# Zero-padded 128x128 operands for the 64-row tails of two attention heads, with an earlier place for a final check

## The chip, the cores and the metric

The kernel runs on one core of one Trainium2 chip. The metric is the device time of one execution in microseconds. TensorE (PE, with its weight loads shown as PEld), VectorE (DVE), ScalarE (ACT) and GpSimd (POOL) each work through their own list of instructions in order and wait for each other through semaphores; DMAs are issued from SyncE's queue (SP).

## The reference

Two blocks follow each other, all in float32. The first is attention with 8 batches, 8 heads, 576 positions and a head size of 64, in which every query keeps only its 32 largest scores. The second is a feed-forward block on the 4608 rows of 512 that come out of it.

```python
scores = scale * np.matmul(q, k.transpose(0, 1, 3, 2))
kth = np.partition(scores, -top_k, axis=-1)[..., -top_k:-top_k + 1]
scores = np.where(scores >= kth, scores, -1000000000.0)
attn = softmax(scores)                      # exp, divided by its sum
x = (attn @ v) as rows of 8 * 64
...
h = x @ w_in                                # 512 -> 1024
solu = h * softmax(h)
ln = (solu - mean) / sqrt(var + 1e-6) * g_ln
out = ln @ w_out                            # 1024 -> 512
```

## The kernel before

The work is cut by pairs of heads. A pair has two heads of 64, so both lie on the 128 partitions, head 0 on partitions 0 to 63 and head 1 on 64 to 127. The 576 positions of a head are four main chunks of 128 (`NM = 4`) and a **tail of 64** (`ST`). The two heads' tails of queries make one tile of 128 rows, so one step has nine tiles of 128 query rows by 576 keys: two for each of four main chunks, and one for the tails of a pair. There are 32 steps, four for each batch, and 32 pairs, four for each batch.

The keys of a pair are prepared once: `load_k` (L664) loads the main keys `km` and the two tails `qt` and `kt`, each with 64 positions on partitions and both heads side by side; `prep_t` (L701) turns the two tails around on PE, `prep_tc` (L711) copies the result to the keys `kT` on ACT (L712, L713); `prep_k` and `prep_kc` do the main keys, `moments` and `moments_c` a matrix from which the spread of the scores is estimated. `load_v` (L678) loads the values, their tails `vt` with head 0 on partitions 0 to 63 and head 1 on 64 to 127.

In a step, `spread` (L782) makes the small products for that estimate, `scores` (L850) the scores in PSUM (`s_ps`, two buffers of two banks), `evac` copies them to SBUF on ACT. Three rounds of counting on DVE and ACT (`count0`, `count1`, `count2`) close in on each row's threshold, `nearest`, `best` and `kth` (L985) find it exactly, `exps`, `keep` and `norm` make the weights, `transpose_p` and `transpose_last` turn them around on PE, `copy_p`, `copy_pt` and `copy_last` bring them to SBUF as `PT`, and `attn_v` (L1083) multiplies them by the values, in two parts: part 0 has 320 query columns (two main chunks and a tail), part 1 has 256. `copy_v` puts the result in place for the feed-forward block: `mm1` (L1117), `hexp`, `solu`, `square`, `ln`, `transpose_ln`, `copy_ln`, `mm2` (L1176), `store` (L1184).

All products that concern heads work on a part of TensorE's array. A main score product contracts 64 rows and fills 128 columns; in the profile's form that is `64*128`, and the two heads' products lie on different halves of the rows. A product of `attn_v` is `128*64`, the two heads on different halves of the columns. The tail products of `scores`, `attn_v` and `spread` are `64*64`, head 0 on one corner of the array and head 1 on the opposite one. A float32 product shows as two records in the trace, a transpose and a bfloat16 product as one.

The order is written out by hand. Every operation is entered with a due time (`at`), from tables: `step_times` (L1199) for a step, `early_times` (L1235) in its place for the first four steps, `key_times` (L1372) for the pairs (the first batch apart), `first_times`, `token_times` and `last_times` for the feed-forward block, `weights_times` (L1463) for the 16 chunks of 128x512 weights. These weights come as 64-bit floats; `load_w`, `w_bits` (DVE), `w_low` (ACT), `w_mul` and `w_add` (POOL) make float32 of them near the start, and `w_again` (a second load), `w_exp` (DVE) and `w_check` (ACT, L631) look near the end whether their exponents were in range. Sorted by due time, the tables give the order of each engine's list (L1546); a due time has no other effect.

Last come a check and a branch: six reductions on DVE (L1557, to `hit` and `ok`) count whether every row met its conditions and every weight its range, a small product and two operations on one number (L1562 to L1568) make one flag of that, `bad`. Every engine loads it, and only if it is set does a general version of the kernel run (L1580).

Lines of the score and value products that can't be said in a sentence:

```python
s = big[0][h * ST : (h + 1) * ST] if tail else big[h]
...
lhsT=vm[:, h, c, :] if c < NM else vt[hd, :],
rhs=pt[:, h * NM + c, :] if c < NM else pt[hd, 2 * NM, :],
start=(c == 0), stop=(c == NM),
```

Of the kernel before, what the change touches and what calls it, by code (L numbers as in the profile page):

```python
# [8 lines left out]
F32 = mybir.dt.float32  # L9
# [434 lines left out]
def fast_path(  # L444
# [98 lines left out]

    def trunc(ap):

        return ap.bitcast(BF16)[:, 1::2]
# [117 lines left out]
    def load_k(n):  # L664
# [9 lines left out]
        for nm, src in (("q", q), ("k", k)):  # L674
            d[nm + "t"] = p1.tile([ST, 2, D], F32, tag=nm + "t", name=nm + "t")
            nc.sync.dma_start(out=d[nm + "t"], in_=src[b, hh, SM:S, :].rearrange("h p d -> p h d"))

    def load_v(n):  # L678
# [3 lines left out]
        t = p4.tile([2 * ST, D], F32, tag="vt", name="vt")  # L682
        nc.sync.dma_start(out=m, in_=v[b, hh, 0:SM, :].rearrange("h (p t) d -> p h t d", t=NM))
        for h in range(2):
            nc.sync.dma_start(out=t[h * ST : (h + 1) * ST, :], in_=v[b, 2 * hp + h, SM:S, :])
        ks[n]["v"] = (m, t)

    def kT_of(n):

        return once(  # L690
            ks[n], "kT", lambda: p4.tile([P, S + 2 * ST], F32, tag="kT", name="kT")
        )
# [8 lines left out]
    def prep_t(n):  # L701

        d = ks[n]
        pre = pre_of(n)
        for m, nm in enumerate("qk"):
            nc.tensor.transpose(
                pre[:, m * ST : (m + 1) * ST], d[nm + "t"].rearrange("p h d -> p (h d)"),
                ident[0:ST, 0:ST],
            )

    def prep_tc(n):  # L711
        nc.scalar.copy(out=kT_of(n)[:, 0 : 2 * ST], in_=ks[n]["pre"][:, 0 : 2 * ST])  # L712
        nc.scalar.copy(out=kT_of(n)[:, S + ST : S + 2 * ST], in_=ks[n]["pre"][:, ST : 2 * ST])  # L713
# [13 lines left out]
    def prep_kc(n):  # L727

        nc.scalar.activation(
            out=kT_of(n)[:, 2 * ST : S + ST], in_=ks[n]["tp"], func=AF.Copy,  # L730
            accum_out=mom_of(n)[:, D : D + 1],
        )

    def moments(n):
        d = ks[n]
        tm = d["tm"] = pre_of(n)[:, 2 * ST : 2 * ST + D]
# [34 lines left out]
    def queries_of(i, c):  # L771

        return keys_of(i, c)["kT"][:, 0:ST] if c == NM else st[i]["qT"][:, c * P : (c + 1) * P]
# [8 lines left out]
    def spread(i):  # L782
# [5 lines left out]
        for c in range(NM + 1):  # L788
            for h in range(2):
                hd = slice(h * D, (h + 1) * D)  # L790
                nc.tensor.matmul(
                    out=d["yt"][h * ST : (h + 1) * ST, :] if c == NM else d["ym"][:, c, h, :],
                    lhsT=trunc(queries_of(i, c)[hd, :]), rhs=trunc(keys_of(i, c)["mom"][hd, :]),
                    start=True, stop=True,
                )

# [53 lines left out]
    def scores(i, t):  # L850
# [3 lines left out]
        tail = t == NM  # L854
        js = [2 * t] if tail else [2 * t, 2 * t + 1]
        big = [ps_big.tile([P, 2, 512], F32, tag="big", name="s_ps") for _ in js]

        for half in range(2):
            for h in range(2):
                hd = slice(h * D, (h + 1) * D)  # L860
                s = big[0][h * ST : (h + 1) * ST] if tail else big[h]

                k0 = ST + half * SH + (ST if h == 0 or tail else 0)
                nc.tensor.matmul(  # L864
                    out=s[:, half, 0:SH], lhsT=queries_of(i, t)[hd, :], rhs=kT[hd, k0 : k0 + SH],
                    start=True, stop=True,
# [170 lines left out]
    def pt_of(i, part):  # L1037

        return once(
            st[i], ("PT", part),  # L1040
            lambda: p2.tile([P, 2 * NM + 1, SP], F32, tag="PT", name="PT"),
# [41 lines left out]
    def attn_v(i, part):  # L1083
        o = st[i]["om", part] = ps_o.tile([P, 512], F32, tag="o", name="om")

        for n, cols in runs_of(i, part):
            vm, vt = keys_of(i, n)["v"]
            pt = pt_of(i, part)[:, :, cols]
            for c in range(NM + 1):
                for h in range(2):  # L1090
                    hd = slice(h * ST, (h + 1) * ST)
                    nc.tensor.matmul(  # L1092
                        out=o[h * D : (h + 1) * D, cols],
                        lhsT=vm[:, h, c, :] if c < NM else vt[hd, :],
                        rhs=pt[:, h * NM + c, :] if c < NM else pt[hd, 2 * NM, :],
                        start=(c == 0), stop=(c == NM),
                    )

# [92 lines left out]

    todo = []
    STEP = 39

    def at(time, f, *args):
# [41 lines left out]
            (load_q, [()], [-136.1]),  # L1237
            (prep_q, [()], [-49.08]),
            (prep_qc, [()], [-46.09]),
            (spread, [()], [-22.56]),  # L1240
# [371 lines left out]
```

## Time and profile before

| | |
|---|---|
| median of four runs | 1288.4 us (1287.45 to 1290.17) |
| the profiled execution's own time | 1289.86 us |
| its span, first to last instruction | 1288.1 us |
| mean granted TensorE clock | 0.968 of full speed |
| kth of steps 0 to 4 (first operation, L990) | 66.8, 98.7, 141.6, 182.8, 218.9 us |
| kth of step 31 | 1196.8 us |
| last record of `o_ps` (L1179) begins | 1275.05 us |
| flag `bad` written (L1565) | 1279.9 us |

The profile is of one execution. A line of a group reads: line of the kernel, engine, operation, written tile and read tiles, the part of the array (rows*columns) for a product, the shape as partitions x elements, and how often. Busy time can overlap, as products are pipelined. The chain that ended last is followed back from the last instruction: at each step to what released it, or to the instruction before it on its engine. From 1280.6 us on, after the branch, nothing but closing of semaphores and queues is left.

### The profile page before, as it was taken

What the parts mean: (1) busy time and instruction counts of PE and PEld (TensorE: products, weight loads), DVE (VectorE), ACT (ScalarE), POOL (GpSimd) and SP (SyncE); (2) the same over time, 40 slices, a digit from 0 to 9 for tenths busy, and PEclk for the clock granted to TensorE, in tenths of its full rate; (3) what the DMA queues carried; (4) which work ended last, traced back from release to release, by engine and by line L of the source; (5) the groups of instructions that cost most, each with busy time, mean ns of one, the idle gap of its engine ahead of it and who ended that gap; (6) DMA issues with size and microseconds to landing.
All of it is one profiled execution on the core that took longest, in us unless ns stands there. A gap on an engine that the chain in (4) does not pass through costs nothing.

```text
span 1288.1 us, 20283 instructions
## 1 busy us (share of the span) xinstructions
PE 1198.8 (93%) x6243; PEld 656.6 (51%) x6243; DVE 1138.0 (88%) x2910; ACT 1130.7 (88%) x2478; POOL 480.1 (37%) x583
## 2 busy tenths in 40 slices
PE   6566889999999999999999999999999999998996
PEld 4233444555554555555554555555555555554442
DVE  5899899999999979999999988999999988999512
ACT  4998897999998989999998989999999889998534
POOL 5546523343443223444442324444432234443310
PEclk9577799999999999999999999999999999999998
DMA  8202110011110121011111021011111011102321
GB/s 239 81 27 71 29 38 28 18 39 37 39 37 21 28 55 39 19 31 36 39 36 28 19 60 35 25 30 29 46 37 26 22 38 27 37 5 77 108 74 61
DMA packets 106245, 56.99 MB, mean 44 GB/s; under 512 B 89224, under 2 KB 97424, under 8 KB 106128
## 3 DMA queue, kind: packets, MB, share of 16 engines
q1 hardware_dynamic: 106128, 55.61, 15.4%
q8 instruction: 52, 0.85, 0.3%
q14 instruction: 65, 0.53, 0.1%
HBM read 46.14 MB, written 9.44 MB: 43 GB/s over the span
## 4 chain that ended last, share of the span: by engine, by line
PE 55%; ACT 20%; DVE 17%; issue 4%; POOL 2%; DMA 1%; SPq 0%; DVEq 0%; ACTq 0%; POOLq 0%
PE o_ps L1179 13%; PE s_ps L864 12%; PE h_ps L1121 11%; PE tp_p L1035 7%; PE om L1092 6%; ACT junka L889 4%; DVE junkv L881 4%; DVE E L1006 4%; ACT sg L941 4%; DVE w L969 3%; DVE w L962 3%; ACT E L977 3%; PE tp_ln L1168 2%; ACT PT L1047 2%; ACT X L873 2%
## 5 line engine op out<-in xcount | busy, mean ns | idle before, releaser
L1179 PE MATMUL o_ps<-w_out,lnT 128*128 128x512 f32 x576 | 263.0, 600 | 0.1
L1021 POOL TENSOR_SCALAR E<-E,rden 128x576 f32<-128x576 f32 x256 | 204.6, 813 | 99.4 <-DVE rden L1017 94.2
L881 DVE TENSOR_SCALAR_CACHE_REDUCE junkv<-X,t 128x576 bf16<-128x576 f32 x280 | 224.4, 802 | 15.6 <-ACT X L873 8.0
L934 POOL TENSOR_SCALAR tt<-t 128x9 f32<-128x9 f32 x32 | 20.8, 650 | 561.0 <-DVE t L929 543.0
L1121 PE MATMUL h_ps<-w_in,xTm 128*128 128x512 f32 x512 | 227.5, 595 | 1.1 <-ACT xTm L1107 1.1
L864 PE MATMUL s_ps<-kT,qT 64*128 64x288 f32 x1024 | 198.9, 463 | 17.4 <-ACT X L873 6.2
L969 DVE MAX8 w<-w 128x8 f32<-128x576 f32 x288 | 210.3, 750 | 0.1
L962 DVE SCALAR_TENSOR_TENSOR w<-X,al,sg 128x576 f32<-128x576 f32 x256 | 210.2, 824 | 0.2
L1006 DVE SCALAR_TENSOR_TENSOR E<-X,kth,E 128x576 f32<-128x576 f32 x256 | 199.1, 815 | 10.2 <-ACT E L977 9.8
L941 ACT ACTIVATE sg<-X,t 128x576 bf16<-128x576 f32 x256 | 196.2, 771 | 0.1
L889 ACT ACTIVATE junka<-X,t 128x576 bf16<-128x576 f32 x232 | 180.3, 777 | 12.7 <-DVE t L912 8.9
L873 ACT ACTIVATE X<-s_ps 128x576 f32<-128x576 f32 x256 | 157.6, 656 | 36.2 <-PE s_ps L864 33.1
L1035 PE MATMUL tp_p<-ident,E 128*128 128x128 f32 x1024 | 154.3, 283 | 16.3 <-POOL E L1021 8.9
L1047 ACT COPY PT<-tp_p 128x512 f32<-128x512 f32 x256 | 147.1, 598 | 22.6 <-PE tp_p L1035 22.5
L1179 PEld LDWEIGHTS o_ps<-w_out,lnT 128*128 128x128 f32 x576 | 104.6, 191 | 110.0 <-issue 107.0
L1035 PEld LDWEIGHTS tp_p<-ident,E 128*128 128x128 f32 x1024 | 115.4, 143 | 85.7 <-issue 39.6
L1121 PEld LDWEIGHTS h_ps<-w_in,xTm 128*128 128x128 f32 x512 | 94.4, 190 | 110.7 <-issue 102.2
L864 PEld LDWEIGHTS s_ps<-kT,qT 64*128 64x128 f32 x1024 | 116.6, 201 | 60.2 <-issue 19.2
L977 ACT ACTIVATE E<-X 128x1152 f32<-128x1152 f32 x128 | 146.7, 1172 | 0.0
L1092 PE MATMUL om<-PT,vm 128*64 128x256 f32 (+1 forms) x1024 | 141.3, 419 | 2.6 <-ACT xTt L1113 2.6
L1092 PEld LDWEIGHTS om<-PT,vm 128*64 128x64 f32 x1024 | 68.9, 139 | 62.0 <-issue 22.2
L829 POOL TENSOR_TENSOR zs<-zs,phalf 128x9 f32<-128x9 f32 x32 | 71.0, 2218 | 2.7
(127 smaller groups left out, 1628.6 us busy)
## 6 DMA issues: line engine op xcount, KB each, us to landing
km<-in_k_dram SPq DMA_DIRECT2D x32, 256.0 KB, 3.2
qm<-in_q_dram SPq DMA_DIRECT2D x128, 64.0 KB, 2.0
vm<-in_v_dram SPq DMA_DIRECT2D x32, 256.0 KB, 2.7
out_dram<-osb SPq DMA_DIRECT2D x32, 256.0 KB, 2.4
w_raw<-in_moe_w_in_dram SPq DMA_DIRECT2D x8, 512.0 KB, 4.7
w_raw<-in_moe_w_out_dram SPq DMA_DIRECT2D x8, 512.0 KB, 3.4
w_again<-in_moe_w_in_dram SPq DMA_DIRECT2D x8, 512.0 KB, 4.3
w_again<-in_moe_w_out_dram SPq DMA_DIRECT2D x8, 512.0 KB, 3.2
```

What stands on the lines that cost most here:

```text
L864: nc.tensor.matmul(out=s[:, half, 0:SH], lhsT=queries_of(i, t)[hd, :], rhs=kT[hd, k0 : k0 + SH], start=True, stop=True,)
L881: nc.vector.tensor_scalar(out=junk, in0=x_of(i, j), scalar1=st[i][t][:, j : j + 1], scalar2=None, op0=ALU.is_ge, op1=ALU.add, accum_out=co ...
L889: nc.scalar.activation(out=junk, in_=x_of(i, j), func=AF.Sign, scale=-1.0, bias=st[i][t][:, j : j + 1], accum_out=columns(i, c)[:, j : j + 1],
L941: nc.scalar.activation(out=d["sg", j], in_=x_of(i, j), func=AF.Sign, scale=-(1.0 + 2.0**-23), bias=d["t2"][:, j : j + 1], accum_out=column ...
L962: nc.vector.scalar_tensor_tensor(out=w, in0=x_of(i, j), scalar=d["al"][:, j : j + 1], in1=d.pop(("sg", j)), op0=ALU.subtract, op1=ALU.mult,)
L969: nc.vector.max(w8[:, j, :], st[i].pop(("w", j)))
L1006: nc.vector.scalar_tensor_tensor(out=e, in0=x_of(i, j), scalar=d["kth"][:, j : j + 1], in1=e, op0=ALU.is_ge, op1=ALU.mult, accum_out=den_a ...
L1021: nc.gpsimd.tensor_scalar(out=e, in0=e, scalar1=st[i]["rden"][:, j : j + 1], scalar2=1.0, op0=ALU.mult, op1=ALU.mult,)
L1035: nc.tensor.transpose(tp[:, c, :], e[:, c * P : (c + 1) * P], ident)
L1092: nc.tensor.matmul(out=o[h * D : (h + 1) * D, cols], lhsT=vm[:, h, c, :] if c < NM else vt[hd, :], rhs=pt[:, h * NM + c, :] if c < NM else ...
L1121: nc.tensor.matmul(out=h[:, half, :], lhsT=x[:, c, :], rhs=w_in[:, c, half * 512 : (half + 1) * 512], start=(c == 0), stop=(c == NP - 1),)
L1179: nc.tensor.matmul(out=o, lhsT=d["lnT"][:, c, :], rhs=w_out[:, c, :], start=(c == 0), stop=(c == NF - 1),)
```

## The change

The tails of both heads are put on the diagonal of 128x128 tiles that are set to zero once, at the start, and one product over the full array takes the place of two on opposite corners.

- Six tiles are added and zeroed by DVE ahead of everything: two `qk_tails` of 128x2x128 and four `v_diag` of 128x128. Pairs use them in turn.
- `load_k` loads the two heads' query tails with one DMA each to the diagonal blocks, and the key tails of both with one DMA to partitions 0 to 63; before it was one DMA for the query tails and one for the key tails, and one buffer each.
- `load_v` puts the value tails on the diagonal of `v_diag`, with two DMAs as before.
- `prep_t` does two transposes of 128x128 instead of two of 64 rows and 128 columns. `prep_tc` copies the query tails to a tile of their own (`qTt`, 128 columns) and the key tails with one operation to both ends of `kT`, which read them twice; `kT` becomes 64 columns shorter, with tail, main, tail.
- `scores` for the tails: two products (one for each half of the keys) instead of four. `spread`: one instead of two. `attn_v`: one for each part instead of two; its main products stay as they are.
- `PT` gets a tag of one buffer for each part, in place of one tag with two buffers.
- The check's reductions and its verdict become `w_passed` and `w_verdict`, with due times of their own in `weights_times` among the end's work; on DVE three of the reductions stand ahead of or among the last `w_exp`, and the order of the reductions changes.
- `early_times`, the first batch's column of `key_times`, `first_times`, `last_times` and `weights_times` get new numbers, so another order in the first four steps and at the end. `step_times`, `token_times`, `tails_times` and the later batches' column stay.

```diff
+    ok = const.tile([P, 6], F32, tag="ok", name="ok")
+    qk_tails = [const.tile([P, 2, P], F32, tag=f"qk_tails{n}", name="qk_tails") for n in range(2)]
+    v_diag = [const.tile([P, P], F32, tag=f"v_diag{n}", name="v_diag") for n in range(4)]
+    for t in qk_tails + v_diag:
+        nc.vector.memset(t, 0.0)
...
-        for nm, src in (("q", q), ("k", k)):
-            d[nm + "t"] = p1.tile([ST, 2, D], F32, tag=nm + "t", name=nm + "t")
-            nc.sync.dma_start(out=d[nm + "t"], in_=src[b, hh, SM:S, :].rearrange("h p d -> p h d"))
+        d["tails"] = qk_tails[n % 2]
+        for h in range(2):
+            hd = slice(h * ST, (h + 1) * ST)
+            nc.sync.dma_start(out=d["tails"][hd, 0, hd], in_=q[b, 2 * hp + h, SM:S, :])
+        nc.sync.dma_start(
+            out=d["tails"][0:ST, 1, :].rearrange("p (h d) -> p h d", h=2),
+            in_=k[b, hh, SM:S, :].rearrange("h p d -> p h d"),
+        )
...
-            nc.sync.dma_start(out=t[h * ST : (h + 1) * ST, :], in_=v[b, 2 * hp + h, SM:S, :])
+            hd = slice(h * ST, (h + 1) * ST)
+            nc.sync.dma_start(out=t[hd, hd], in_=v[b, 2 * hp + h, SM:S, :])
...
-        for m, nm in enumerate("qk"):
+        for m in range(2):
             nc.tensor.transpose(
-                pre[:, m * ST : (m + 1) * ST], d[nm + "t"].rearrange("p h d -> p (h d)"),
-                ident[0:ST, 0:ST],
+                pre_of(n)[:, m * P : (m + 1) * P], ks[n]["tails"][:, m, :], ident
             )
...
-        nc.scalar.copy(out=kT_of(n)[:, 0 : 2 * ST], in_=ks[n]["pre"][:, 0 : 2 * ST])
-        nc.scalar.copy(out=kT_of(n)[:, S + ST : S + 2 * ST], in_=ks[n]["pre"][:, ST : 2 * ST])
+        nc.scalar.copy(out=qT_of(n), in_=pre[:, 0:P])
+        nc.scalar.copy(
+            out=kT_of(n).rearrange("p (a c) -> p a c", c=ST)[:, 0 :: S // ST, :],
+            in_=pre[:, P : P + ST].unsqueeze(1).broadcast_to([P, 2, ST]),
+        )
...
+        nc.tensor.matmul(
+            out=d["yt"], lhsT=trunc(queries_of(i, NM)), rhs=trunc(keys_of(i, NM)["mom"]),
+            start=True, stop=True,
+        )
...
-            for h in range(2):
-                hd = slice(h * D, (h + 1) * D)
-                s = big[0][h * ST : (h + 1) * ST] if tail else big[h]
-                k0 = ST + half * SH + (ST if h == 0 or tail else 0)
+            for h in range(len(js)):
+                hd = slice(0, P) if t == NM else slice(h * D, (h + 1) * D)
+                k0 = half * SH + (ST if h == 0 else 0)
...
-            for c in range(NM + 1):
+            for c in range(NM):
                 for h in range(2):
-                    hd = slice(h * ST, (h + 1) * ST)
                     nc.tensor.matmul(
-                        out=o[h * D : (h + 1) * D, cols],
-                        lhsT=vm[:, h, c, :] if c < NM else vt[hd, :],
-                        rhs=pt[:, h * NM + c, :] if c < NM else pt[hd, 2 * NM, :],
-                        start=(c == 0), stop=(c == NM),
+                        out=o[h * D : (h + 1) * D, cols], lhsT=vm[:, h, c, :],
+                        rhs=pt[:, h * NM + c, :], start=(c == 0), stop=False,
                     )
+            nc.tensor.matmul(
+                out=o[:, cols], lhsT=vt, rhs=pt[:, 2 * NM, :], start=False, stop=True
+            )
...
-            (load_q, [()], [-136.1]),
+            (load_q, [()], [-111.2]),
...
-        (load_k, [-186.91, -84.21, -66.88, -51.07], [-71.77, -54.35, -34.54, -26.23]),
-        (load_v, [55.06, 17.62, 49.21, 80.2], [46.71, 33.98, 89.74, 55.28]),
-        (prep_t, [-76.64, -32, -22.27, 26.83], [-50.7, -40.81, -7.18, 29.61]),
+        (load_k, [-151.18, -97.4, -60.66, -21.5], [-71.77, -54.35, -34.54, -26.23]),
+        (load_v, [50.1, 2.95, 59.43, 22.63], [46.71, 33.98, 89.74, 55.28]),
+        (prep_t, [-65.39, -32.79, -5.4, 17.24], [-50.7, -40.81, -7.18, 29.61]),
...
-        (store, [()], [204.61]),
+        (store, [()], [169.03]),
...
-            -264.91, -138.71, -79.38, -78.33, -63.45, -50.94, -40.81, -7.68, -10.19, -32.43,
+            -266.59, -157.62, -119.88, -90.6, -77.8, -34.85, -27.64, 1.31, -20.84, -63.29,
...
+        (w_passed, True, range(6), [
+            215.56, 235.59, 242.57, 269.1, 243.49, 241.78,
+        ]),
+        (w_verdict, True, range(1), [
+            280.18,
+        ]),
```

## The prediction

> **What bounds the kernel now.** I read the busy table first, then busy time by stretch, the chain that ended last, and TensorE's timeline of one step.
>
> ```profile
> PE 1198.8 (93%) x6243; PEld 656.6 (51%) x6243; DVE 1138.0 (88%) x2910; ACT 1130.7 (88%) x2478; POOL 480.1 (37%) x583
> ```
> ```profile
> 32.00:100.00 68.00, 40.87 (x214) 23.27 (x212) 62.38 (x149) 66.42 (x148) 31.95 (x32) 0.69 0.20 56
> ...
> 300.00:1180.00 880.00, 867.70 (x4644) 477.53 (x4643) 829.36 (x2152) 819.66 (x1789) 321.12 (x395) 1.00 0.13 34
> ```
> ```profile
> PE 55%; ACT 20%; DVE 17%; issue 4%; POOL 2%; DMA 1%; SPq 0%; DVEq 0%; ACTq 0%; POOLq 0%
> ```
> The columns of the second fence are the stretch, its length, busy PE, PEld, DVE, ACT, POOL, the granted clock, the DMA share and GB/s. From 300 to 1180 us PE is busy 98.6%, DVE 94%, ACT 93%: three nearly equal loads in fixed orders, and the chain changes hands between them. From 32 to 100 us ACT leads with 98%. So a microsecond saved on PE counts only where PE is on the chain, and not in the first 100 us. The chain's old length, less what is saved on it, stays a floor as long as the order stays; so the on-chain saving is the most that the products can bring.
>
> TensorE's timeline (start, length, engine, line, operation) shows the places that change:
>
> ```profile
> 704.80 3.60 PE L1179 MATMUL o_ps<-w_out,lnT 128*128 128x512 f32 x8
> 708.24 0.60 PE L1035 MATMUL tp_p<-ident,E 128*128 128x128 f32 x4
> 708.77 1.24 PE L864 MATMUL s_ps<-kT,qT 64*128 64x288 f32 x8
> 709.94 0.66 PE L1168 MATMUL tp_ln<-ident,solu 128*128 128x128 f32 x4
> ...
> 717.25 1.09 PE L1035 MATMUL tp_p<-ident,E 128*128 128x128 f32 x8
> 718.28 1.19 PE L864 MATMUL s_ps<-kT 64*64 64x288 f32 x8
> 719.39 0.66 PE L1035 MATMUL tp_p<-ident,Et 128*128 128x128 f32 x4
> ```
> ```profile
> 679.37 2.37 PE L1092 MATMUL om<-PT,vm 128*64 128x320 f32 x16
> 681.67 0.76 PE L1092 MATMUL om<-PT,vt 64*64 64x320 f32 x4
> 682.36 1.95 PE L1092 MATMUL om<-PT,vm 128*64 128x256 f32 x16
> 684.24 0.65 PE L1092 MATMUL om<-PT,vt 64*64 64x256 f32 x4
> 684.82 0.66 PE L719 MATMUL tp_qk<-ident,qm 128*128 128x128 f32 x4
> ```
> I use slots: from a group's start to the next group's start. The eight o_ps records take 3.44 us, so a record of 512 columns takes 0.429 us, 0.84 ns a column; a float32 product is two records. The tail scores are eight records of 288 columns; one after the other they would take 8 × 0.242 = 1.93 us, yet their slot is 1.11. So the two heads' 64x64 products **already run side by side**: four record times, 0.97 us. One full-array product per half also takes four record times. The change saves no streaming; what it can save is what surrounds a packed group.
>
> That surround is measurable between 300 and 1180 us, where slots repeat within a few ns. The o_ps group takes 3.435 us between full-array groups, 3.529 if the next group is packed, 3.537 if the one before was, 3.632 if both. A group of four transposes takes 0.436, 0.530, 0.492 and 0.585. The main scores take 1.171 before a full-array group but 1.074 before another group of the same 64*128 packing. So going into a packed group costs 0.094, coming out 0.097 in its own slot plus 0.056 (transposes) or 0.10 (o_ps) in the next.
>
> **The change part by part, per step of 36.6 us (293 us for eight).**
>
> *Tail scores*, between transposes: before 1.023 + 1.118 + 0.492; after 0.929 + 0.966 + 0.436. That is −0.30 us; between 0, if the full-array group pays as much itself, and −0.30.
>
> *prep_t*, two transposes of 64 columns in a 64*128 group of 0.264 us: after, two of 128 columns at 0.109 each, 0.218. Between full-array groups (16 of 22 places) it saves 0.046 + 0.094 + 0.056 to 0.10, about 0.21. In the six places behind main scores it loses, as the packing is left a step earlier: 0.097 + 0.066 − 0.056 = +0.107. Mean −0.12; ends −0.21 and 0.
>
> *Spread tail*: slot 0.148 for two small bf16 products behind others of the same packing; the way out moves ahead of the new product. I take −0.10, ends 0 and −0.15.
>
> *attn_v tails*: slots 0.686 and 0.580 for 0.537 and 0.430 of streaming, an excess of 0.15 each. But the products before them stay 128*64, so a full-array tail makes a new way out (0.097 + 0.056 to 0.10) and, in the first part, a new way in (0.094): first part +0.10 to +0.14, second −0.05 to −0.01 with its successor's 0.056. I take **+0.09** for both; ends +0.135, and −0.355 if the new product pays nothing.
>
> "TensorE: Matmul & The Clock Gate" (Measured speedup vs the span model) of the Trainium skill speaks against the whole change: a packed span is the product's length plus about 4 ns per further tile. By it, nine pairs a step would save 36 ns, an estimate of 1.2 us in 32 steps. The side-by-side streaming agrees, but the trace's 0.15 us of excess a group does not. "TensorEngine Tiling (Array Packing)" (Key Properties) says that changing the mode drains the array, which fits 0.094 in and 0.097 out; it would let 128*64 to 64*64 cost as much, and there the slots (2.304 and 1.877 us, the same excess at both sizes) show nothing extra.
>
> What lies on the chain: in the chain in order of time, the attn_v tails are on it in 15 of 32 steps, the tail scores in 9, prep_t for about 45% of its time (14.5), the spread tail in 15. So 9 × −0.30 − 14.5 × 0.12 − 15 × 0.10 + 15 × 0.09 = −2.7 − 1.8 − 1.5 + 1.35 = **−4.6 us**. Ends: 9 × 0.30 + 23 × 0.21 + 15 × 0.15 + 15 × 0.355 = −15 (prep_t has a place in 23), and +2 if only attn_v's loss is real.
>
> *ACT*: prep_tc's second copy (0.245) becomes one of 128 elements with a repeated read, nearest row 0.283: 32 × 0.038 = 1.2 us, on the chain with ACT's 20%: **+0.25**, ends 0 and 1.2.
>
> *Loads*: one more DMA a pair, 0.6 us of issue on SP's queue; what is behind it are later loads, and after 7.6 us SP issue isn't on the chain: 0. The q and k tails get two buffers each, so qt waits for the transposes of two pairs back. The v tails keep four, and PT keeps one buffer a part. Six memsets are new on DVE, none shown; at most the 0.43 of a 128x512 operation, 2.6 us in all. DVE waits for its first weights until 4.53 us, which hides them; without that cover they would hold the first tail loads behind km on SP, up to 0.7 us.
>
> *Start*: the chain there is:
>
> ```profile
> 7.62 3.37 DMA km<-in_k_dram
> ...
> 12.16 5.00 DMA qt<-in_q_dram
> ...
> 17.20 0.55 PE pre L706 x2
> 17.75 2.08 PE s_ps L864 x8
> ```
> prep_t of pair 2 stands ahead of the first scores on PE and waits for qt until 17.16. The new order puts it behind them, so that wait goes. Late next is pair 1, whose loads now stand behind one more weight chunk and two more tail DMAs: issue from 7.62 + 2 × 0.62 to 12.1, landing 2.1 later at the median and up to 5.0 as here, then 1.5 us of transposes and copies: first scores between 15.7 and 18.6 against 17.49. Midpoint: **−0.4**. Pair 3 also moves behind three weight chunks (512 KB each, 2.2 us at the 238 GB/s of the first 32 us) and a q load; its kT copy is due only at 34.8 us. For the rest of the reordered first four steps no row gives a sign: 0. Bound: their last two intervals between kth are 42.9 and 41.2 us against 36.1 later, 11.9 us to win, and as much to lose.
>
> *End*: PE stands 0.95 us before its last products because o_ps waits for the osb copy, which ACT runs behind weight checks; ACT now copies earlier. The check's six reductions (1277.01 to 1279.23) are already the end's path, and the new order still puts two weight checks behind the last osb copy and five reductions behind those: about +0.55. The last store issues at 1276.84 and takes 2.3, so under the check lies only 0.8 us. Together **−0.4**, ends −1.4 and +0.6.
>
> Sum: −4.6 + 0.25 − 0.4 − 0.4 = −5.2 us. The profiled execution took 1289.86 us, 1.8 outside its span of 1288.1; it is 1.5 above the median of 1288.4. Its forecast is 1284.7; for the median, **1283.2**.
>
> **Rivals.** *Nothing moves*: the packed pairs already share the array, and where PE arrives earlier it waits for ACT to empty the two score buffers (the main scores take 1.37 at the median, 1.17 at best). For it: ACT and DVE at 93 to 94%. Against: stretches such as 450 to 500 us, where the chain is PE alone. It gives 1288.4 + 0.25 − 0.8 = 1287.9. *Slower*: the new order of the first four steps makes ACT stand. It idles 1.6 + 8.8 = 10.3 us between 32 and 183; doubled, that gives 1283.2 + 10.3 = 1293.5, and it decides from 7.8 us on. For it: ACT at 98% has no slack, and three weight chunks move ahead of pair 3. Against: pair 3 has some 8 us of cover. *More*: full-array groups pay nothing anywhere, or the early steps lose their excess: 1288.4 − 15 = 1273.4, or 1283.2 − 11.9 = 1271.3.
>
> **Chances.** Forecast (1280 to 1285.8) 0.45; more 0.20; nothing 0.17; slower 0.18. A difference under 0.2% (2.6 us) can't be told from none. Faster is forecast plus more, 0.65. The range, 1272 to 1293, leaves out the outer half of the slower case and the far end of the larger gain.
>
> **What would show it.** Tail scores as four records in about 0.97 us, the transposes around them at 0.93 and 0.44; prep_t in 0.22; attn_v's tails with a full-array record and the slots of both parts together longer by about 0.09; steady intervals of 35.1 us falling by 0.1 to 0.3; the first s_ps between 15.7 and 18.6 us; PE without the 0.95 us wait at the end. I am wrong if steady intervals stay, if attn_v's slots shorten by 0.3, or if kth of step 4 (218.9 us now) moves by more than 5 us.

## The result and the profile after

The changed kernel takes **1290.88 us** (median of 33 runs, 1288.64 to 1295.31) against 1288.77 for the kernel before in the same rounds: ratio **1.0021**, 95% interval 1.0016 to 1.0025. It is slower by 0.2%; 1283.2 was forecast. The profiled spans are 1289.2 and 1288.1 us.

Busy times of the changed kernel (first part of its page), then the same two stretches as before, then the shares of its chain:

```profile
PE 1187.2 (92%) x5955; PEld 672.7 (52%) x5955; DVE 1148.4 (89%) x2916; ACT 1131.5 (88%) x2478; POOL 482.0 (37%) x583
```
```profile
32.00:100.00 68.00, 42.09 (x170) 25.09 (x172) 61.61 (x141) 61.15 (x137) 33.06 (x32) 0.62 0.21 60
300.00:1180.00 880.00, 859.83 (x4444) 490.31 (x4442) 832.39 (x2160) 821.73 (x1796) 320.94 (x394) 1.00 0.12 32
```
```profile
PE 46%; ACT 28%; DVE 19%; issue 4%; POOL 2%; DMA 1%; SPq 0%; DVEq 0%; ACTq 0%; POOLq 0%
```

PE is busy 11.6 us less, as meant, and the chain left it for ACT (its share falls from 55% to 46%, ACT's rises from 20% to 28%). The time did not follow. Two rows say why: between 32 and 100 us ACT, which had 66.42 of 68 us of work before, has only 61.15, so it stands; and from 300 to 1180 us PE is busy 7.9 us less, while the steps end hardly earlier.

The span can be cut at two marks that every version has, the first operation of `kth` of step 4 and of step 31, into start, middle and end:

| us | start | middle | end |
|---|---|---|---|
| before | 218.9 | 977.9 | 91.3 |
| after | 225.2 | 975.6 | 88.4 |
| difference | **+6.3** | −2.3 | −2.9 |

So middle and end came 5.2 us shorter, and the first four steps took 6.3 more. Not all of the 2.9 at the end belongs to the change's parts: behind the flag `bad`, where only the branch and the closing of queues are left, the span runs on for 8.1 us before and 6.5 after. The kths of steps 0 to 4 lie at 70.1, 105.5, 150.0, 190.0, 225.2, where they were at 66.8, 98.7, 141.6, 182.8, 218.9: the loss is there after step 1.

The places shown of the timeline before, in the changed kernel (start, length, engine, line, operation):

```profile
722.05 1.09 PE L1054 MATMUL tp_p<-ident,E 128*128 128x128 f32 x8
722.98 1.14 PE L883 MATMUL s_ps<-kT,qTt 128*128 128x288 f32 x4
723.95 0.60 PE L1054 MATMUL tp_p<-ident,Et 128*128 128x128 f32 x4
```
```profile
684.64 2.37 PE L1111 MATMUL om<-PT,vm 128*64 128x320 f32 x16
686.94 0.81 PE L1115 MATMUL om<-PT,v_diag 128*128 128x320 f32 x2
687.68 1.95 PE L1111 MATMUL om<-PT,vm 128*64 128x256 f32 x16
689.56 0.70 PE L1115 MATMUL om<-PT,v_diag 128*128 128x256 f32 x2
690.09 0.60 PE L737 MATMUL tp_qk<-ident,qm 128*128 128x128 f32 x4
690.53 7.03 PE L1141 MATMUL h_ps<-w_in,xTm 128*128 128x512 f32 x16
```

The tail scores' slot, start to next start, is 723.95 − 722.98 = 0.97 us, and the eight transposes ahead take 0.93 (1.11 and 1.03 in the lines of before). In `attn_v` the two tails and the transposes behind take 0.74 + 0.53 + 0.44 = 1.71 us, where the lines of before give 0.69 + 0.58 + 0.49 = 1.76; the main products keep their slots of 2.30 and 1.88 in both.

The chain at the start of the changed kernel:

```profile
9.76 3.20 DMA km<-in_k_dram
...
13.09 1.94 PE tp_qk L737 x8
...
16.90 0.40 PE y_ps L809 x8
17.30 0.17 PE y_ps L813
17.47 7.08 PE s_ps L883 x17
```

The wait for `qt` is gone from it, and the main keys of pair 1, issued at 9.76 instead of 7.62, take its place: the first scores come at 17.4 us, as they did before.

### The profile page after: what moved, and what is told of

Read it like the earlier page. It is cut to its first block, busy times and chain, and to the rows that moved or that the text cites. A ratio compares the mean times of both kernels' runs of the same rounds, so it can differ in the third digit from the quotient of the medians.

```text
span 1289.2 us, 19758 instructions
## 1 busy us (share of the span) xinstructions
PE 1187.2 (92%) x5955; PEld 672.7 (52%) x5955; DVE 1148.4 (89%) x2916; ACT 1131.5 (88%) x2478; POOL 482.0 (37%) x583
## 4 chain that ended last, share of the span: by engine, by line
PE 46%; ACT 28%; DVE 19%; issue 4%; POOL 2%; DMA 1%; SPq 0%; DVEq 0%; ACTq 0%; POOLq 0%
PE s_ps L883 12%; PE o_ps L1199 11%; PE h_ps L1141 8%; PE tp_p L1054 7%; ACT junka L908 6%; ACT sg L960 5%; DVE E L1025 5%; DVE junkv L900 4%; ACT E L996 4%; PE om L1111 3%; DVE w L988 3%; ACT PT L1067 3%; DVE w L981 3%; PE tp_ln L1188 2%; ACT X L892 2%
## 5 line engine op out<-in xcount | busy, mean ns | idle before, releaser
L981 DVE SCALAR_TENSOR_TENSOR w<-X,al,sg 128x576 f32<-128x576 f32 x256 | 213.7, 836 | 0.3
L892 ACT ACTIVATE X<-s_ps 128x576 f32<-128x576 f32 x256 | 158.4, 656 | 32.9 <-PE s_ps L883 31.9
```

What stands on the lines that cost most here:

```text
L981: nc.vector.scalar_tensor_tensor(out=w, in0=x_of(i, j), scalar=d["al"][:, j : j + 1], in1=d.pop(("sg", j)), op0=ALU.subtract, op1=ALU.mult,)
```

## The experiments

### Which part of the change loses the time

Four kernels take the change apart into three parts: its operands, its start order (the tables of the first four steps, of the first batch's keys and of the weights) and its end (last tables and the check's place). With the old start order the two tail buffers need the tail loads of pair 3 behind the transposes of pair 1, so they become an operation of their own, `load_t`.

```diff
-            (load_q, [()], [-111.2]),
+            (load_q, [()], [-136.1]),
...
-        (load_k, [-151.18, -97.4, -60.66, -21.5], [-71.77, -54.35, -34.54, -26.23]),
+        (load_k, [-186.91, -84.21, -66.88, -51.07], [-71.77, -54.35, -34.54, -26.23]),
+        (load_t, [-186.91, -84.21, -66.88, -31.9], [-71.77, -54.35, -34.54, -26.23]),
```

New operands and new end, old start order:

> The new operands and the new end, with the first four steps (and the first batch's loads, weights and feed-forward rows) in the order of before; only the tail loads of pair 3 are issued later, behind the transposes of pair 1. Theory A, the new start order loses the time: kth of step 4 near 219 to 220 us instead of 225.2, the whole about 5 us under before, ratio 0.995 to 0.997. Theory B, the new operands themselves slow the start (three tail DMAs a pair, 128-column transposes): kth of step 4 stays near 225 us and the ratio near 1.002.

New operands alone:

> The new operands alone: start order, end order and the check's place as before (tail loads of pair 3 behind the transposes of pair 1). Theory A: the middle gains about 2.3 us (kth of step 4 to kth of step 31 in 975.6 instead of 977.9 us), the start nothing, the end little; ratio about 0.998. Theory B: ratio about 1.004, kth of step 4 near 225 us.

New start order alone, on the old operands:

> The kernel before with the new order of the start alone. Theory A: it loses some 6 us, kth of step 4 near 225 us, ratio 1.004 to 1.006. Theory B: the order is harmless without the new operands, ratio 0.999 to 1.001, kth of step 4 near 219 us.

New end alone:

> The kernel before with the new order of the end and the check among the last products. If the order brings the end's gain (from kth of step 31 to the end 91.3 us before, 88.4 after): ratio about 0.998 and 88 to 89 us. If the gain comes from the operands or from elsewhere: ratio 1.000, and 91 us.

| kernel | ratio to before (95%) | start | middle | end |
|---|---|---|---|---|
| operands and end | 0.9969 (0.9960 to 0.9978) | 219.3 | 975.2 | 88.0 |
| operands | 0.9984 (0.9975 to 0.9993) | 219.6 | 975.6 | 89.6 |
| start order | 1.0061 (1.0044 to 1.0078) | 222.0 | 978.7 | 91.4 |
| end | 1.0000 (0.9991 to 1.0009) | 218.2 | 977.4 | 90.5 |

Start, middle and end are read from one profiled execution of each kernel. With the new operands kth of step 4 lies 0.7 and 1.1 us later (219.6 against 218.9, 219.3 against 218.2), which can't be told from scatter: in six kernels with the new operands and the same old order up to kth of step 0, that mark alone lies anywhere between 66.3 and 68.1. The start order alone makes the kernel slower: 1295.20 us against 1287.95, 7.3 us by the medians. Its profiled execution took 1293.91, so the marks show only a part of that. On the new operands and the new end the same order costs 0.52% (1.0021 against 0.9969), 6.7 us. The theory that the operands (more loads, buffers in turn) slow the start fell. **Operands and end with the old start order take 1284.09 us** against 1287.95 in the same rounds: this version beats both kernels.

### Why the products bring so little

The expected −4.6 us supposed that PE is often what ends a step. Between the same two kths, of step 4 and of step 31, PE's idle time grew from 16.3 to 26.9 us (first before, then after): of 12.9 us less work 10.6 became waiting.

```profile
218.90:1196.80 977.90, 961.59 (x5149) 528.39 (x5147) 924.12 (x2388) 911.29 (x1991) 359.36 (x438) 1.00 0.13 34
225.20:1200.80 975.60, 948.71 (x4912) 541.53 (x4911) 925.30 (x2389) 910.54 (x1990) 359.27 (x438) 1.00 0.13 34
```

The intervals between kths repeat every eight steps: before 35.1 five times, 39.6, 36.0, 41.9; after 35.1 five times, 39.1, 35.9, 41.8. Only the long steps moved: −0.7 us in eight, −2.3 in the 27 of the middle. A 35.1, a 39 and a 41.8 step of the changed kernel, by engine (columns as above), and last a 35.1 step of before:

```profile
588.80:623.90 35.10, 34.72 (x195) 20.28 (x194) 34.30 (x90) 34.07 (x77) 13.07 (x16) 1.00 0.16 43
694.20:733.20 39.00, 38.31 (x205) 22.12 (x204) 36.38 (x94) 35.43 (x80) 13.76 (x19) 1.00 0.13 33
769.20:811.00 41.80, 41.42 (x223) 23.72 (x220) 34.22 (x91) 39.03 (x86) 13.11 (x16) 1.00 0.21 56
583.50:618.60 35.10, 34.86 (x203) 19.82 (x202) 34.30 (x91) 34.18 (x77) 13.03 (x16) 1.00 0.16 43
```

PE looks fullest in each. But DVE has 34.30 us of work in a step of 35.10, and 34.30 before as well: as long as DVE's gaps stay, nothing that PE saves makes such a step shorter. To tell the binding engine, one engine at a time got more work. One more tile of the second count on DVE instead of ACT:

```diff
-        return 0 if i < FEW else 2
+        return 0 if i < FEW else 3
```

> New operands, old start, new end, with one more tile of the second count on DVE and one less on ACT from step 4 on: DVE +0.88 us a step, ACT -0.97. Theory A (DVE binds the 35.1 us steps): they become 36.0 us, 2.5 us more in a batch of four with its five of eight steps, the whole 13 to 24 us longer than the same kernel without it, 1297 to 1308. Rival (ACT, also at 97%, binds them): no longer, or some us shorter.

The tail scores computed twice, the second over the first (nothing else changes):

```diff
-        for half in range(2):
+        for half in (0, 1, 0, 1) if t == NM else range(2):
```

> New operands, old start, new end, and the tail scores computed twice into the same PSUM buffer: TensorE +0.97 us in each of 32 steps. Theory A (TensorE has slack in five of eight steps): the 35.1 us steps grow by under 0.4 us, the 39.1, 35.9 and 41.8 us steps by 0.7 to 1 us each, the whole by 10 to 18 us, to 1294 to 1302. Theory C (TensorE binds everywhere): all steps grow by 0.97 us, the whole by 27 to 31 us.

The kernel with more on DVE has ratio 1.0065 (1.0050 to 1.0081), the one with more on PE 1.0064 (1.0049 to 1.0079), but in different steps. More on DVE, a 35.1 and the 41.8 step; then more on PE, a 35.1 and the 39.1 step:

```profile
622.50:658.50 36.00, 34.18 (x171) 18.97 (x170) 35.17 (x93) 32.86 (x73) 13.59 (x16) 1.00 0.13 35
769.40:809.80 40.40, 40.03 (x214) 23.08 (x213) 35.00 (x92) 38.01 (x83) 13.08 (x16) 1.00 0.21 56
```
```profile
590.20:625.40 35.20, 34.96 (x196) 20.63 (x195) 34.36 (x91) 33.91 (x76) 12.78 (x16) 1.00 0.16 42
695.70:736.40 40.70, 40.70 (x212) 23.38 (x211) 35.87 (x95) 35.61 (x80) 13.78 (x19) 1.00 0.13 31
```

With 0.87 us more on DVE the short step grows by 0.8 to 0.9, and the long one, whose ACT was relieved, shrinks from 41.8 to 40.4 or less: DVE sets the five short steps, ACT the longest. With about 1 us more on PE the short steps stay at 35.1 to 35.3, the 41.8 step at 41.9 in all but one case (42.3), the 39.1 step grows by 1.5 and the 35.9 step by 0.8: PE sets **two steps of eight**, and only there can its saving show.

If that is so, a lighter DVE should let more of the saving through. Both kernels with the new end, old and new operands, got the same relief: `keep` over 320 of 576 columns (the other 256 stay unmasked, so the output is not the reference's) and four tiles of the second count on DVE instead of two.

```diff
-        return 0 if i < FEW else 2
+        return 0 if i < FEW else 4
...
-        e = p_of(i, j)
+        e = p_of(i, j)[:, 0:320]
...
-            out=e, in0=x_of(i, j), scalar=d["kth"][:, j : j + 1], in1=e,
+            out=e, in0=x_of(i, j)[:, 0:320], scalar=d["kth"][:, j : j + 1], in1=e,
```

> Old operands, old start, new end, with less work on DVE and ACT: the masking of the weights (keep) covers 320 of 576 columns, so 256 columns stay unmasked in the output, and from step 4 on two more tiles of the second count go from ACT to DVE. DVE's 34.3 us of a 35.1 us step should become about 32.8, ACT's 34.1 about 32.1. Theory A (five of eight steps are bound by DVE at 34.3 of 35.1 us busy): these steps fall below 35.1 us, to about 33.5 to 34.5, and the whole by 8 to 30 us, ratio 0.977 to 0.994. Theory C (TensorE is the bound in all steps): the steps stay near 35.1 us and the whole within 5 us.

> The same lightening (keep over 320 of 576 columns, two more count tiles on DVE) with the new operands, old start, new end. Theory A: with DVE and ACT out of the way the products' saving of about 0.4 us a step comes through, 8 to 14 us less than light_old. Theory C, or a theory in which the saving is lost in waits for PSUM buffers whatever DVE does: about 4 us less than light_old, as between the full kernels.

Old operands 1276.59 us (ratio 0.9911, 0.9894 to 0.9927), new operands 1267.10 (0.9835, 0.9818 to 0.9851): the operands are now worth 9.5 us, where they were worth 3.8 without the relief (1287.9 and 1284.09). In the middle alone they are worth 7.1 us (967.8 to 960.7) instead of 2.2 (977.4 to 975.2). The eight steps take 290.4 and 288.4 us, and again the short ones are equal (34.4); the three long ones fall by 1.1, 0.4 and 0.6 us. My estimate of the relief was too large, though: DVE is still busy 33.53 of 34.40 us there. So the pair shows that relief of DVE and ACT together lets more of the saving through, in the three long steps alone; how much a free DVE would let through in the short ones it does not show.

### Where in the start the time is lost

First, each half of the new start order with the other half of the old: new weights' tables, then new steps' and keys' tables.

> New operands, new end, old start order, but with the weights' loads and conversions at their new due times (one or two more weight chunks ahead of the first keys). If the weights' places cost the start its 6 us: kth of step 4 near 225 us, ratio near 1.002. If it is the order of the steps' own work: kth of step 4 near 219 us, ratio near 0.997.

> New operands, new end, the new start order for the first four steps, the first batch's keys and feed-forward rows, but the weights' loads and conversions at their old due times. If the order of the steps' own work costs the 6 us: kth of step 4 near 225 us, ratio near 1.002. If the weights' places do: near 219 us, ratio near 0.997.

Ratios 1.0127 (1.0110 to 1.0144) and 1.0098 (1.0081 to 1.0114), kth of step 4 at 236.2 and 238.6: each half alone is far worse than both (the profiled execution of the second took 1303.56 us, 2.8 above its median, so its marks are a little late). In the first ACT stands 10.2 us between 32 and 100 us for POOL's work on the weights, in the second 8.7 for scores. The halves only fit each other, so this cut says nothing on where the loss lies; both theories missed.

Next, the most visible wait of the changed kernel: PE stands 7.3 us at 65.2 us, with half a tile of scores done, since DVE reads the spread of step 2 (`spread_v`, which frees the other PSUM buffer) only behind kth of step 0. The reading was put ahead:

```diff
-            (spread_v, [()], [-18.07]),
-            (spread_r, [()], [-11.45]),
+            (spread_v, [()], [-22.1]),
+            (spread_r, [()], [-22.05]),
```

> The changed kernel with step 2's spread_v and spread_r moved ahead on DVE, from behind step 0's kth to between its last best and nearest operations; TensorE's scores of step 2 wait 7.3 us there for the PSUM buffer that spread_v frees. If this wait starves ACT (its idle time between 32 and 100 us is 6.8 us against 1.6 before): ACT idles 2 to 4 us less, kth of step 4 comes 1.5 to 4 us earlier than 225.2, the whole 1 to 3 us under the changed kernel. If the start's loss lies elsewhere: kth of step 4 within 1 us of 225.2.

Ratio 1.0029 (1.0018 to 1.0039), kth of step 0 at 71.8, of step 4 at 226.3. PE's wait for DVE fell from 7.26 to 1.76 us, but the next wait took its place, for ACT to empty a buffer, and ACT stood as long as before (7.28 us between 32 and 100 us, 6.85 in the changed kernel):

```profile
76.10 1.33 PE L883 MATMUL s_ps<-kT,qT 64*128 64x288 f32 x2 [6.83 <-ACT X L892]
```

This wait of PE was no cause of the loss.

Then a cut in time. The list of each engine follows the new start order up to a due time and the old one from there (or the reverse), so each piece keeps its own order. The operands and the end are the new ones, and due time 60 is about kth of step 0. In short:

```diff
-        for _, _, f, args in sorted(todo, key=lambda x: x[:2]):
+        for _, _, f, args in [x for x in new if x[0] < -22] + [x for x in old if not_yet(x)]:
```

> New operands and new end; the order follows the new start tables for every operation due before -22 (up to the first scores of step 0, about 17 us on the chip) and the old ones for the rest. Known: kth of step 4 at 219.3 us with the old start order, 225.2 with the new one. Theory H, the loss is made before the first scores (the new order has ACT wait 3.0 us with the column of gains ahead of the first weights): kth of step 4 at 223 to 226, ratio to the kernel before about 1.001. Theory M, it is made between the first scores and kth of step 1 (105.5 against 98.7 us): kth of step 4 at 219 to 221, ratio about 0.997 to 0.998. Theory F, the two orders fit only as wholes: above 226, ratio above 1.003.

> As the run that changes the order at -22, but the new tables hold up to due time 20 (before the second count of step 0). H: 223 to 226 for kth of step 4. M: a part of the loss, 220 to 224, and more than with the change at -22. F: above 226.

> As the two runs before, with the new tables up to due time 60, about kth of step 0. H: 223 to 226 for kth of step 4. M: 222 to 226, more than with the change at 20 by 1 to 3 us; kth of step 0 at 70 as in the changed kernel. F: above 226.

> The other way about: the old start order for everything due before -22, the new one from there. H: kth of step 4 at 219 to 221, ratio 0.997 to 0.998. M: 223 to 226, ratio about 1.001. F: above 226, ratio above 1.003.

| start order | kth of step 0 | of step 1 | of step 4 | ratio (95%) |
|---|---|---|---|---|
| old | 67.9 | 99.7 | 219.3 | 0.9969 (0.9960 to 0.9978) |
| new to −22 | 72.0 | 103.9 | 223.5 | 1.0010 (1.0000 to 1.0020) |
| new to 20 | 72.9 | 104.7 | 225.6 | 1.0015 (1.0005 to 1.0024) |
| new to 60 | 69.6 | 102.6 | 222.8 | 1.0009 (0.9999 to 1.0018) |
| new from −22 | 69.8 | 104.9 | 224.5 | 1.0050 (1.0033 to 1.0067) |
| new (the changed kernel) | 70.1 | 105.5 | 225.2 | 1.0021 (1.0016 to 1.0025) |

The marks are again of one execution each, and that of the new order from −22 took 1290.21 us, 3.6 below the median of its four: its ratio says more than its marks.

The changed kernel is ahead at its first scores (17.4 us against 18.9 with the old order) and loses 2.3 us by kth of step 0 and 3.6 more in step 1. That is the stretch of theory M, but M's numbers for the changes at −22 and 20 missed. For the first the reason can be read: joining two orders has a cost of its own. The order that is new only to −22 has the transposes of a later pair ahead of the first scores, as in the kernel before, and they wait for loads that the new order issues later:

```profile
22.54 0.66 PE L726 MATMUL pre<-ident,qk_tails 128*128 128x128 f32 x2 [4.33 <-DMA qk_tails<-in_q_dram]
23.13 2.29 PE L888 MATMUL s_ps<-kT,qT 64*128 64x288 f32 x8
```

Its first scores come at 23.1 us, 4.2 later than with the old order, and its kth of step 4 is 4.2 later too. So this kernel met theory H's number by a wait that the changed kernel does not have. The order that is new from −22 has its first scores at 19.0, as with the old one, and kth of step 0 1.9 us later (69.8; the six kernels with the old order have 66.3 to 68.1): those 2 us are made behind the first scores.

Step 1 takes 31.8 to 31.9 us with the old order behind −22 or 20, 33.0 with it behind 60, and 35.2 and 35.4 in the two kernels that follow the new order to the end. In the same stretch of each kernel, 13 to 33 us behind its own kth of step 0, the old order, the new order up to 60, the new order from −22 and the whole new order show:

```profile
80.90:100.90 20.00, 14.75 (x100) 8.87 (x99) 19.70 (x43) 19.58 (x42) 9.36 (x10) 0.93 0.14 41
```
```profile
82.60:102.60 20.00, 14.95 (x100) 9.00 (x100) 19.90 (x42) 19.41 (x41) 10.61 (x11) 0.93 0.14 41
```
```profile
82.80:102.80 20.00, 17.20 (x98) 11.05 (x96) 18.20 (x36) 17.09 (x37) 10.14 (x10) 0.80 0.09 28
```
```profile
83.10:103.10 20.00, 17.20 (x96) 11.04 (x94) 17.96 (x35) 16.84 (x37) 10.23 (x11) 0.79 0.08 28
```

ACT, which leads in this stretch, is nearly full with the old order behind 60 and stands 2.9 to 3.2 us with the new one, and the granted clock (the 0.93 and 0.80) is lower with it. What ACT waits for in the changed kernel (waits by line; total, times, longest), and PE's timeline there:

```profile
ACT X L892 <- PE s_ps L883: 3.3, 3, 2.4
ACT sg L960 <- DVE t L948: 1.2, 1, 1.2
```
```profile
75.42 1.32 PE L883 MATMUL s_ps<-kT,qT 64*128 64x288 f32 x2 [0.72 <-ACT X L892]
79.49 5.31 PE L883 MATMUL s_ps<-kT,qT 64*128 64x288 f32 x14 [2.75 <-ACT X L892]
84.73 1.97 PE L1054 MATMUL tp_p<-ident,E 128*128 128x128 f32 x8
```

ACT waits for scores; the scores had waited for ACT to empty a buffer, which in the new order stands behind three counts of ACT (76.5 to 78.7 us) whose thresholds `t` came 1.2 us late from DVE. The main scores of one chunk (eight records) then take 2.08 us instead of the 1.17 of later steps; the granted clock is at 0.50 until about 91 us, in the kernel before it is full from 80 us.

Rows of three other stretches bear on the question whether the lower clock makes the loss. First the 13 us behind kth of step 0 with the old order and in the changed kernel, then both stretches with the new start order on the old operands, where step 1 takes 34.4 us (31.9 in the kernel before):

```profile
67.90:80.90 13.00, 7.25 (x31) 4.89 (x32) 12.42 (x44) 12.86 (x29) 5.85 (x8) 0.50 0.11 24
70.10:83.10 13.00, 7.19 (x18) 3.87 (x20) 12.59 (x44) 10.15 (x23) 5.81 (x7) 0.50 0.10 23
```
```profile
70.20:83.20 13.00, 7.25 (x19) 3.88 (x21) 12.59 (x44) 10.09 (x23) 5.87 (x8) 0.50 0.11 24
83.20:103.20 20.00, 16.45 (x108) 9.96 (x104) 18.84 (x37) 17.66 (x38) 10.14 (x10) 0.92 0.09 28
```

In the first 13 us the clock is 0.50 with either order, and ACT stands 0.1 us with the old and 2.9 with the new one. In the next 20 us the kernel of the last row has nearly the mean clock of the old order (0.92 and 0.93), and its ACT still stands 2.3 us and its step 1 is 2.5 us longer. So ACT's standing begins with the order, at an equal clock. How much the later rise of the clock adds is not separated: it comes some 16 us behind kth of step 0 there, 21 in the changed kernel and 11 to 14 in the kernel before and with the old order.

To test it directly, idle products were to keep PE busy in its 7.3 us gap:

```diff
+        for _ in range({2: 36}.get(i, 0)):
+            nc.tensor.matmul(out=d["yt"], lhsT=ident, rhs=ident[:, 0 : D + 1], start=True, stop=True)
```

> The changed kernel with 36 idle float32 products of the unit matrix (128x128 by 65 columns) on TensorE ahead of step 2's small products, at about 63.4 us, where TensorE then stands 7.3 us; what they write is written over by the real products. In the changed kernel the granted clock stays 0.50 until 88 us and the main scores at 72 to 84 us take 2.08 instead of 1.17, and ScalarE waits for them (idle 4.7 us between 80 and 100); in the kernel before the clock is 1.00 from 80 us. Theory K, the low clock makes the loss of step 1: clock 0.8 to 1 between 72 and 84, ScalarE idle under 2 us between 80 and 100, kth of step 1 at 101 to 103.5 instead of 105.5, of step 4 at 221 to 223.5 instead of 225.2, ratio 0.998 to 1.0005. Theory R, the order of the work alone makes it (the transposes of step 0 come at 84.7 instead of 76.7) and the clock is only its sign: kth of step 1 within 0.7 of 105.5, ratio 1.001 to 1.003.

The control with the old start order, and the same with a second place:

> The control: the same idle products at the same place in the kernel with new operands and new end but the old start order, where TensorE stands 7.2 us ahead of step 2's small products (73.65) and ScalarE is idle only 0.4 us between 80 and 100. K and R alike: the clock rises earlier (1.00 by 76 to 80 instead of 81), but no engine waits for it: kth of step 1 at 99 to 100.3 (99.7 without), ratio 0.996 to 0.998 (0.997 without).

> As the control, with 22 more idle products ahead of step 3's small products at 96.8, in front of TensorE's wait of 2.6 us. Without them the clock falls to 0.50 between 100 and 114 and ScalarE is idle 3.4 us between 104 and 116, most of it waiting for scores. K: clock 0.8 to 1 in 100 to 112, ScalarE idle there under 1.5 us, kth of step 2 at 140.5 to 142 (142.9 without), ratio 0.994 to 0.997, the fastest of all kernels here with the whole computation. R: kth of step 2 within 0.7 of 142.9, ratio 0.997.

Ratios 1.0063 (1.0046 to 1.0080), 1.0073 (1.0057 to 1.0090) and 1.0103 (1.0086 to 1.0119). These runs don't decide: I sized the fill wrongly. I took 0.11 us a record from 0.84 ns a column at full clock; the 72 records of the 36 products take 15.6 us, 0.217 each. Every product also loads 128x128 weights, and PEld is busy nearly all that time. So the idle products ran past the gap and stood on the path: kth of step 1 at 112.4, 115.4 and 115.2 us. And they don't raise the clock (stretches of the first of the three):

```profile
62.00:78.00 16.00, 16.00 (x82) 15.72 (x82) 9.60 (x23) 13.13 (x28) 0.00 (x0) 0.50 0.00 1
88.00:96.00 8.00, 7.30 (x26) 4.67 (x26) 7.83 (x15) 4.55 (x10) 8.00 (x10) 0.50 0.17 66
98.00:100.00 2.00, 2.00 (x14) 1.73 (x13) 1.10 (x3) 1.71 (x4) 1.90 (x2) 0.91 0.01 4
```

**What stays open:** how much the later rise of the clock adds to the loss of step 1, and which operations make the 2 us before kth of step 0. What is shown is that both losses come from the start order, the second mostly from what it lists behind due time 60, and that ACT then stands, for late thresholds and for scores.

## Why the prediction was wrong, step by step

- **"For the rest of the reordered first four steps no row gives a sign: 0".** This step decided the sign: +5.9 us by kth of step 4 between the new and the old start order (225.2 against 219.3; the rest is the same but for the place of pair 3's tail loads). There was a sign: ACT was busy 98% from 32 to 100 us with an order in which nearly every operation found its input ready. Such an order can be changed to no gain worth having and to a loss of many us, so "11.9 us to win, and as much to lose" was not symmetric. The slower rival named the mechanism, ACT standing: its idle time between 32 and 183 us went from 10.3 to 14.4, and is 8.8 with the new operands and the old start order: 5.7 us of difference beside the 5.9 lost. I gave it 0.18, with a threshold that counted only the start's loss against a gain that was itself too large.
- **"First scores between 15.7 and 18.6"**: right, 17.4. But an earlier first score did not carry to kth of step 0 (70.1 against 66.8); "−0.4" was +3.3 by then.
- **"−4.6 us" on the chain**: −2.3 in the middle. The slots were right: tail scores 0.973 (0.966 expected), transposes around them 0.929 and 0.436, `prep_t` 0.218. What failed is the count of places where they matter. The prediction calls the on-chain saving the most that the products can bring, and then takes it as what they will bring: it read 98.6% busy as PE binding, and in the short steps DVE binds. So 10.6 of the 12.9 us of work that left PE between kth of steps 4 and 31 became waiting. The Trainium skill warns of this reading in its page "Perfetto Trace Analysis" (its opening): busy time of matmuls is a bad measure, as they are pipelined. The runs agree: PE is busy 34.72 of 35.10 us in a step that 1 us more of PE work leaves at 35.1 to 35.3. The rival "nothing moves" had this cause, with ACT's buffers as the place rather than DVE.
- **`attn_v` +0.09 a step**: −0.05. I expected a way out of the packing in the main products' slots; their slots (2.30 and 1.88) did not change, and only the first tail takes longer (0.69 to 0.74), while the second and the transposes behind take 0.04 and 0.06 less.
- **Spread tail −0.10 a step**: about −0.12. Its slot falls from 0.148 to 0.040 and that of the `o_ps` group behind from 3.537 to 3.516, while the products ahead take 0.007 more.
- **ACT +0.25 and loads 0**: nothing speaks against them. The four memsets of 128x128 take 0.165 us each, the two of 128x256 take 0.27, 1.2 in all, under DVE's first wait as supposed.
- **End −0.4**: −2.9, in three parts. From kth of step 31 to the end of the last `o_ps` it is 0.6 less (78.8 to 78.3): the 0.95 us was the wait of the weight load PEld, not of PE, whose last 24 records took 10.85 us before and take 10.46 now, 0.39 less. From there to the flag it is 0.6 less (4.3 to 3.7): 0.80 us of reductions follow the last weight check, where 2.23 stood at the end before (1277.01 to 1279.24). The new end alone has 0.4 and 0.6 of these. The largest part, 1.7 us, lies behind the flag (8.1 to 6.5), where no term of the sum looks. There the four kernels with the old operands have 8.1 to 9.0 us and 14 of the 16 with the new ones 5.8 to 6.7, but the other two have 7.9 and 8.9; why is open.
- **"What would make it wrong"** named the right marks: kth of step 4 moved by 6.3 us, more than the 5 set there, and the steady intervals of 35.1 us stayed.

## What to carry to other kernels

Before a saving on one engine is counted, split the steady state into its single steps and set each engine's busy time against that step's length; an engine within 2 or 3% of it in most steps caps the gain there, however busy another looks. A change that comes with a new hand-written order is two changes: price the order by the engine that is already full in it, where a reorder has much to lose and little to win, and try the rest of the change on the old order. Here that gives 1284.1 us against 1288.0 for the kernel before in the same rounds; the changed kernel takes 1290.9.

## What the runs showed of the hardware

- 36 float32 products (72 records) of 65 columns with full 128x128 weights kept PE busy for 15.6 us without a gap, and the granted clock stayed at 0.50; it came to 0.91 only at 98 us, among scores and transposes. The page "TensorE: Matmul & The Clock Gate" (What's actually happening) of the Trainium skill has the gate open after about 3.4 us of busy PE. By that it would have been open by about 69 us (an estimate: two such windows from 62 us on); here busy time alone did not open it, and the measurement decides. What the gate counts is not shown.
- Such a product takes 0.217 us a record at half clock, against an estimate of 0.11 from its columns (65 columns at twice 0.84 ns). The weight load is busy 15.72 of the same 16.00 us, so the weights set its pace as far as the profile shows.
- Behind the 128*64 products of `attn_v` a full-array tail costs less than a 64*64 one where full-array work follows, and more where another 128*64 group does. The slot of the products ahead of the second tail is 1.88 us with either. That tail takes 0.536 us for 0.430 of streaming and the transposes behind it 0.436; before they took 0.580 and 0.492. The first tail, ahead of another 128*64 group, grows from 0.686 to 0.736.
